# Reordering the step list of an attention and token-mixing kernel so that the steps of more batches are interleaved

## The chip, the cores and the metric

The kernel runs on one core of one Trainium2 chip. The metric is the device time of one execution in microseconds (us). Some words are used throughout. PE is TensorE's matrix unit and PEld its weight loads, DVE is VectorE, ACT is ScalarE, POOL is GpSimd, SP is SyncE. "Granted clock" is the share of full speed that the profile shows as granted to PE; in the clock records it is only ever 1.0 or 0.5 at any one moment. These records begin at about 34 us of the span before, and what lies before counts as full clock in every mean and row below. It was not: the eight `pq` transposes of batch 0 took 1.97 us, as at half clock (in the middle of the run they take 1.94 us at half clock). A timed run is 1.7 to 2.0 us longer than the span of instructions that its profile shows (one run 2.8), so spans are compared with spans and times with times. Runs are marked fast or slow (slow: over 1.5% above the fastest of the same kernel); only fast runs are compared.

## The reference

For each of 8 batches, 8 heads, 576 positions and head size 64, an attention with two parts is computed, and a token-mixing layer follows it.

```python
q_d, k_d, v_d = means over groups of 4 positions            # 144 coarse positions
out_d   = softmax(scale * q_d @ k_d.T) @ v_d                # coarse attention
out_up  = repeat(out_d, 4)                                  # back to 576 positions
local   = softmax(scale * q @ k.T where |i-j| < 4) @ v      # band attention
x       = (out_up + local) as (8, 576, 512)

wq, wk  = x @ w_q, x @ w_k                                  # 512 -> 64
W_tok   = wq @ wk.T / 8                                     # 576 x 576 per batch
out     = relu(W_tok @ x) @ w_out                           # 512 -> 512
```

## The kernel before

Each batch is cut into about forty small steps. A step issues a few instructions on one or several engines and hands its results on in a dictionary. The parts of a batch, in the order in which they depend on one another, with the names that the profile shows:

- `load_qk`, `load_v`: DMA of q, k, v. `cast_qk`, `cast_v`: casts to 16 bits, on GpSimd (for batch 0 q and k are cast on DVE and ACT).
- `tq`, `tk`, `tr`: transposes on PE (`pq`, `pk`, `pr`), copied to `qT`, `kT`. `sums`: sums over groups of 4 of `qT` and `kT`, on GpSimd.
- `mask`, `score`: band scores (`psc`), then `E = exp` on ACT. `av`: E times v (`pav`), normalised by DVE into `x`.
- `vd`, `cs`, `ca`: the coarse attention (`pv`, `pcs`, `pca`, with `Ec = exp` on ACT and `od` on DVE). `xt`, `odt`: transposes of x and od (`px`, `pod`).
- `wtd`, `wt`, `wkt`, `wks`, `m2`: the small products of the mixing layer (`pwd`, `pw`, `pwk`, `pws`, `pm`). `mx`: the mixing with relu (`pmx`, into `rmx`). `og`, `ol`: the output projections (`po`, `pol`), copied to `os`, `ol` and sent to memory.

Two things make the order of the steps matter. First, the program keeps the instructions of every engine in the order in which it issues them:

```python
class _InOrder:
    # ... cut ...
    def __getattr__(self, name):
        f_ = getattr(self._engine, name)
        return lambda *a, **k: self._tc.keep_in_program_order(f_(*a, **k))
```

Every instruction goes through the line with `keep_in_program_order`, which is why the profile gives L27 for nearly all of them; groups are told apart by their tiles. Second, the order is one list of (lag, step). In iteration i the step is run for batch i + lag:

```python
    ORDER = [
        (-2, "og1"), (-1, "wtd"), (0, "sums"), (1, "cast_qk"), (-1, "wt"), (0, "vd"), (0, "mask0"),
        (0, "score0"), (-1, "wks"), (2, "load_qk"), (1, "cast_v"), (0, "mask1"), (-1, "wkt"), (0, "score1"),
        (0, "mask2"), (0, "av0"), (-1, "m2"), (0, "av3"), (0, "score2"), (0, "av1"), (-1, "mx0"), (-1, "mx1"),
        (0, "av2"), (0, "cs0"), (-1, "mx2"), (0, "cs1"), (0, "av4"), (0, "weights"), (-1, "mx3"), (1, "tq"),
        (0, "ca0"), (2, "load_v"), (-1, "og0"), (0, "ca1"), (1, "tk"), (1, "tr"), (-1, "ol"), (0, "xt0"),
        (0, "xt1"), (0, "odt"),
    ]
    # ... cut ...
    for i in range(-3, B + 3):
        for lag, name in ORDER:
            if 0 <= i + lag < B and (i + lag, name) not in done:
                steps[i + lag][name]()
```

PSUM, where PE writes its results, has three rotating buffers for the large results and two for the small ones, so a PE group also waits until the group three before it has been read out (in the trace before, `pmx` waits seven times for DVE's `x` and six times for ACT's `E`, 4.1 and 3.6 us in all, and reads neither):

```python
    ps2 = ctx.enter_context(tc.tile_pool(name="ps2", bufs=3, space=bass.MemoryType.PSUM))
    ps1 = ctx.enter_context(tc.tile_pool(name="ps1", bufs=2, space=bass.MemoryType.PSUM))
```

The softmax here doesn't subtract the row's maximum and nothing guards it: scores larger than these inputs give would overflow.

## Time and profile before

| | before |
|---|---|
| time, median of the first three runs | 211.77 us (211.1 to 213.29) |
| span of the profiled run | 208.9 us |
| mean granted clock of that span | 0.909 |
| PE busy | 165.1 us of 208.9 |
| one batch in the middle of the run | about 22.3 us |

The page of the profiled run gives the busy time of each engine over the whole span, then rows with the busy share, in tenths, of 40 equal slices of the span (here 5.2 us each), then the chain of work that ended last, by engine. In the group line, the last column is the engine's idle time before that group and what ended it.

```profile
PE 165.1 (79%) x2768; PEld 110.7 (53%) x2768; DVE 106.5 (51%) x252; ACT 98.9 (47%) x141; POOL 114.9 (55%) x114
...
PE   0260889778998699959996899789986999699690
...
POOL 6005961998489907991299629970799167000000
PEclk9999999995799889985999699957998899859999
...
PE 59%; DVE 13%; POOL 8%; ACT 7%; SPq 6%; issue 3%; DMA 2%; POOLq 0%; ACTq 0%; DVEq 0%
...
L27 POOL TENSOR_TENSOR sum<-qT 128x1152 f32<-128x1152 f16 x8 | 16.9, 2114 | 37.7 <-ACT qT L27 37.7
```

PE is the busiest engine and the first of the chain, but the row of its clock has a dent once per batch: digits of 5 to 8 are slices in part of which the clock was halved. GpSimd idles 37.7 us for `qT`, because its sums stand right behind the transposes of their batch.

The view of chosen stretches has, for each stretch, its bounds and length, the busy time and the number of instructions of PE, PEld, DVE, ACT and POOL, then the granted clock, the DMA share and GB/s. The first two lines are two stretches of about a batch each; the others cut up one thin stretch and what follows it.

```profile
82.80:105.30 22.50, 20.08 (x346) 13.42 (x345) 11.94 (x24) 11.56 (x18) 14.19 (x14) 0.85 0.81 220
105.30:127.40 22.10, 19.51 (x351) 13.53 (x349) 12.01 (x25) 11.62 (x18) 15.97 (x14) 0.92 0.85 226
88.80:92.20 3.40, 1.61 (x56) 0.81 (x44) 2.96 (x6) 1.39 (x3) 3.40 (x3) 1.00 1.01 409
...
92.40:99.20 6.80, 6.24 (x55) 4.09 (x48) 3.38 (x8) 3.19 (x4) 2.60 (x2) 0.51 0.95 155
```

In the 3.40 us before 92.2, PE is busy 1.61 us, a share of 0.47. For the 6.8 us after it the clock is 0.51. The busy time of PE in a batch (20.08 and 19.51) thus contains work that ran at half speed.

The timeline of PE over this place shows start, duration, tile and count of each group, and in brackets the idle time before it and what ended that.

```profile
89.59 0.28 PE L27 MATMUL pmx<-wT,M 64*128 64x288 f16 x1 [0.59 <-ACT E L27]
90.11 0.29 PE L27 MATMUL pmx<-wT,M 64*128 64x288 f16 x1 [0.24 <-DVE M L27]
91.06 0.30 PE L27 MATMUL pmx<-wT,M 64*128 64x288 f16 x2 [0.67 <-DVE x L27]
91.29 0.32 PE L27 MATMUL pav<-v,E 64*64 64x65 f16 x16
91.91 0.59 PE L27 MATMUL pcs<-qd,kd 64*128 64x168 f16 x12 [0.29 <-DVE x L27]
...
94.88 1.94 PE L27 MATMUL pq<-id,q 128*128 128x128 f32 x8
```

Small groups stand here one behind another. Most wait for a PSUM buffer that DVE or ACT has yet to read out: the waits of 0.59, 0.67 and 0.29 us at 89.59, 91.06 and 91.91 ended with `E` and `x`, which read PSUM and are no inputs of these groups (the `pmx` at 90.11 waits for its input M). The eight `pq` transposes that follow take 1.94 us; at full clock in the same trace the eight `pk` transposes take 1.07 us.

### The profile page before, as it was taken

The page shows a single profiled execution, that of the slowest core. Times are in us where ns is not written, and L with a number is a line of the kernel's source. Part 1 is how long each engine was busy: PE and PEld are TensorE (multiplying, and loading weights), DVE is VectorE, ACT ScalarE, POOL GpSimd, SP SyncE. Part 2 cuts the span into 40 slices and gives each one's busy share as a digit, 9 for nine tenths or more (in the row PEclk, how much of TensorE's full clock was granted, in tenths as well). Part 3 has the DMA queues.
Part 4 walks back from the last instruction along what each step waited for, and adds up shares of the span by engine and source line. Part 5 has one row for each costly group of instructions (what it writes and reads, how often), then busy time and mean ns, then how long its engine had stood idle before and what let it go on. Part 6 is the DMA issues. An engine that isn't in the chain of part 4 may idle for free.

```text
span 208.9 us, 6392 instructions
## 1 busy us (share of the span) xinstructions
PE 165.1 (79%) x2768; PEld 110.7 (53%) x2768; DVE 106.5 (51%) x252; ACT 98.9 (47%) x141; POOL 114.9 (55%) x114
## 2 busy tenths in 40 slices
PE   0260889778998699959996899789986999699690
PEld 0240568546664476626763676356653776346330
DVE  4609464565345734574447445673458345644230
ACT  2170573445456445553574546544665346614231
POOL 6005961998489907991299629970799167000000
PEclk9999999995799889985999699957998899859999
DMA  6999999969969999898659995996220053002216
GB/s 199 335 178 334 387 162 284 311 128 295 301 121 317 369 186 245 250 346 137 180 145 386 154 221 147 346 240 134 104 104 3 0 151 107 0 3 100 100 38 213
DMA packets 53290, 40.53 MB, mean 194 GB/s; under 512 B 43984, under 2 KB 44048, under 8 KB 53264
## 3 DMA queue, kind: packets, MB, share of 16 engines
q1 hardware_dynamic: 53184, 40.12, 71.7%
q8 instruction: 21, 0.34, 0.7%
q14 instruction: 5, 0.04, 0.1%
q10 hardware_dynamic: 80, 0.03, 0.1%
HBM read 30.67 MB, written 9.44 MB: 192 GB/s over the span
## 4 chain that ended last, share of the span: by engine, by line
PE 59%; DVE 13%; POOL 8%; ACT 7%; SPq 6%; issue 3%; DMA 2%; POOLq 0%; ACTq 0%; DVEq 0%
PE po L27 14%; PE pq L27 7%; DVE x L27 6%; SPq L27 6%; PE pm L27 5%; PE pca L27 5%; PE psc L27 4%; PE pk L27 3%; PE pw L27 3%; PE px L27 3%; ACT Ec L27 2%; PE pws L27 2%; PE pav L27 2%; DMA w<-in_moe_w_q_dram 2%; POOL v L27 2%
## 5 line engine op out<-in xcount | busy, mean ns | idle before, releaser
L27 POOL TENSOR_TENSOR sum<-qT 128x1152 f32<-128x1152 f16 x8 | 16.9, 2114 | 37.7 <-ACT qT L27 37.7
L27 PE MATMUL po<-wo,rmx 128*128 128x512 f16 x128 | 34.9, 420 | 0.1
L27 POOL CAST v<-v 128x2560 f16<-128x2560 f32 x8 | 18.6, 2326 | 20.7 <-DMA w<-in_moe_w_q_dram 13.6
L27 ACT COPY os<-po 128x1024 f32<-128x1024 f32 x16 | 16.2, 1013 | 28.4 <-PE po L27 21.8
L27 DVE TENSOR_TENSOR x<-pav,rz 128x512 f16<-128x512 f32 x40 | 27.7, 692 | 1.4
L27 PE MATMUL pq<-id,q 128*128 128x128 f32 x64 | 15.8, 426 | 10.9 <-DVE q L27 9.4
L27 PEld LDWEIGHTS <-rmx 128*128 128x128 f16 x144 | 14.4, 107 | 16.2 <-issue 5.0
L27 ACT ACTIVATE E<-psc 128x928 f16<-128x928 f32 (+1 forms) x24 | 19.3, 806 | 4.5 <-PE psc L27 3.8
L27 POOL CAST q<-q 128x1152 f16<-128x1152 f32 x14 | 20.2, 1490 | 0.0
L27 POOL CAST k<-k 128x1152 f16<-128x1152 f32 x14 | 20.2, 1482 | 0.0
L27 PEld LDWEIGHTS pq<-id,q 128*128 128x128 f32 x64 | 12.4, 223 | 12.9 <-DVE q L27 9.4
L27 PE MATMUL pmx<-wT,M 64*128 64x288 f16 x64 | 11.2, 322 | 10.2 <-DVE x L27 4.1
L27 ACT ACTIVATE Ec<-pcs 128x1008 f16<-128x1008 f32 (+1 forms) x16 | 13.9, 873 | 10.8 <-PE pcs L27 10.8
L27 PE MATMUL pav<-v,E 64*64 64x65 f16 x640 | 15.1, 207 | 2.4 <-issue 0.9
L27 PEld LDWEIGHTS <-E 64*64 64x64 f16 x640 | 11.6, 116 | 9.3 <-issue 5.5
L27 DVE RECIPROCAL rc<-pca 128x8 f32<-128x8 f32 (+1 forms) x16 | 3.2, 203 | 25.1 <-PE pca L27 25.1
L27 POOL TENSOR_TENSOR sum<-kT 128x1152 f32<-128x1152 f16 x7 | 14.7, 2106 | 0.5
L27 DVE RECIPROCAL rz<-pav 128x8 f32<-128x8 f32 x40 | 8.1, 203 | 12.4 <-PE pav L27 12.2
L27 PEld LDWEIGHTS <-Ec 128*128 128x128 f16 x160 | 12.3, 122 | 4.1 <-issue 0.8
L27 ACT COPY qT<-pq 128x1024 f32<-128x1024 f32 x8 | 8.1, 1012 | 13.3 <-PE pq L27 13.3
L27 DVE TENSOR_TENSOR wT<-pw,wTd 128x576 f16<-128x576 f32 x8 | 6.1, 758 | 14.4 <-ACT wTd L27 12.9
L27 ACT ACTIVATE rmx<-pmx 128x576 f16<-128x576 f32 x16 | 10.3, 648 | 4.8 <-PE pmx L27 4.8
(79 smaller groups left out, 316.5 us busy)
## 6 DMA issues: line engine op xcount, KB each, us to landing
v<-in_v_dram SPq DMA_DIRECT2D x80, 128.0 KB, 6.2
q<-in_q_dram SPq DMA_DIRECT2D x8, 1152.0 KB, 7.4
k<-in_k_dram SPq DMA_DIRECT2D x8, 1152.0 KB, 10.9
out_dram<-os SPq DMA_DIRECT2D x16, 512.0 KB, 3.3
wo<-in_moe_w_out_dram SPq DMA_DIRECT2D x2, 512.0 KB, 10.5
out_dram<-ol SPq DMA_DIRECT2D x8, 128.0 KB, 2.6
w<-in_moe_w_q_dram SPq DMA_DIRECT2D x1, 128.0 KB, 4.6
w<-in_moe_w_k_dram SPq DMA_DIRECT2D x1, 128.0 KB, 4.4
```

The lines of the kernel that those rows point to most:

```text
L27: return lambda *a, **k: self._tc.keep_in_program_order(f_(*a, **k))
```

## The change

The intent is to give every group of PE work of another batch to stand between it and its consumer, so that PE, DVE, ACT and GpSimd wait less for each other. No instruction is added or removed. The step list is rewritten: the output projections now come one to three batches further behind the casts than before, the other steps lie in between, and the lags run from +2 to -4 instead of +2 to -2.

```diff
     ORDER = [
-        (-2, "og1"), (-1, "wtd"), (0, "sums"), (1, "cast_qk"), (-1, "wt"), (0, "vd"), (0, "mask0"),
-        (0, "score0"), (-1, "wks"), (2, "load_qk"), (1, "cast_v"), (0, "mask1"), (-1, "wkt"), (0, "score1"),
-        (0, "mask2"), (0, "av0"), (-1, "m2"), (0, "av3"), (0, "score2"), (0, "av1"), (-1, "mx0"), (-1, "mx1"),
-        (0, "av2"), (0, "cs0"), (-1, "mx2"), (0, "cs1"), (0, "av4"), (0, "weights"), (-1, "mx3"), (1, "tq"),
-        (0, "ca0"), (2, "load_v"), (-1, "og0"), (0, "ca1"), (1, "tk"), (1, "tr"), (-1, "ol"), (0, "xt0"),
-        (0, "xt1"), (0, "odt"),
+        (-1, "mask2"), (-1, "score2"), (-4, "ol"), (-2, "vd"), (-2, "av4"), (-2, "cs0"), (-3, "m2"),
+        (-2, "cs1"), (-2, "av2"), (-4, "og0"), (-3, "mx1"), (-2, "ca0"), (-3, "mx0"), (0, "tq"), (-2, "ca1"),
+        (0, "tk"), (-1, "sums"), (-2, "xt0"), (1, "cast_qk"), (2, "load_qk"), (-3, "mx3"), (-2, "odt"),
+        (-1, "mask0"), (-1, "score0"), (-2, "xt1"), (1, "load_v"), (0, "cast_v"), (0, "weights"), (-3, "mx2"),
+        (0, "tr"), (-2, "wtd"), (-1, "mask1"), (-1, "score1"), (-1, "av0"), (-2, "wt"), (-1, "av3"),
+        (-3, "og1"), (-2, "wkt"), (-1, "av1"), (-2, "wks"),
     ]
-    for i in range(-3, B + 3):
+    for i in range(-6, B + 6):
```

In three steps `if i == 0` became a test whether the tile exists already, so that a tile shared by sister steps is made by whichever of them comes first.

More of the change, by code (lines that the diff above doesn't have):

```diff
@@ L376, in f_ @@
                 Ec = EcS[b % 2]
-                if i == 0:
+                if "rc" not in g_:
                     g_["rc"] = big.tile([128, 2, 2, 4], FP32, name="rc", tag="rc")
@@ L414, in f_ @@
             def f_():
-                if i == 0:
+                if "rz" not in g_:
                     g_["rz"] = big.tile([128, NW, 2, 4], FP32, name="rz", tag="rz")
@@ L441, in f_ @@
             def f_():
-                if i == 0:
+                if "xT" not in g_:
                     g_["xT"] = big.tile([128, 4, 2, 290], FP16, name="xT", tag="xT")
```

## The prediction

> **What bounds the kernel now.** In the middle of the run a batch takes about 22.3 us (stretches 82.8 to 105.3 and 105.3 to 127.4 of the view by stretches). TensorE (PE) is busy 20.1 and 19.5 us of these, VectorE about 12, ScalarE 11.6, GpSimd 14 to 16. PE bounds it, but not at its own speed. Each batch has a thin stretch: around the pav, pmx and pcs groups PE waits for VectorE's x or ScalarE's E, and its busy share falls to 0.28, 0.29, 0.65 in three successive microseconds (89 to 92). The granted clock then drops to 0.5 for 3.4 or 6.8 us, by turns (period means 0.92 and 0.85); the pq transposes and an output projection fall in it (8 pq 1.94 us, 8 pk at full clock 1.07). [...]
>
> **What the change does.** Nothing is added or removed; the same 2768 matmuls stand in another order. Each scores, av, mx, coarse and projection group now has work of another batch, ready an iteration earlier, between it and its consumer. Transposes no longer wait for the same iteration's casts; GpSimd's sums wait for a qT that is an iteration old (now it idles 6 to 8 us per batch for it).
>
> **Cost.** Per batch PE's work at full clock, an estimate from start-to-start times in full-clock stretches, is 17.4 us (busy 19.5 to 20.1 less half of the throttled part). GpSimd needs 15.9. DMA: loading one batch takes 15 to 16.5 us from its first packet to its last, its outputs some 3 more, so 18 to 19 if they do not overlap. I estimate 18 to 19 us a batch in place of 22.3, 2 to 2.5 of it from the clock, 1.5 from waits. Half-clock stretches should become rare in the middle.
>
> Given back at the ends: first, GpSimd casts q and k of batch 1 before v of batch 0, and PE has transposes of batch 1 queued ahead of most of batch 0: after the first scores it should idle from about 15 to about 30 us. And the last batch drains over four thin iterations (last pq to end some 53 us; now 47.5). Together 8 to 10 us lost, against six or seven periods times 4 saved.
>
> **Prediction.** Stringing the new queue orders with the trace's durations gives a span near 191 us, so about 193 us timed (timed runs lie 2 to 3 us above the span). Range 185 to 203. Faster by over 2%: 0.94; within: 0.05; slower: 0.01.
>
> **What would show it.** Mean granted clock in the middle 0.93 or more; period between successive pq groups 18 to 19.5 us; GpSimd over 80% busy in the middle, its wait for qT gone; PE busy time down to about 150 us; PE idle 13 us or more before 35 us; loads done by about 130 us instead of 146.
>
> **What would make it wrong.** DMA: if q, k, v loads and outputs slow each other, the period goes to 20 to 21 and the time over 203; then PE or GpSimd waits for in_q or in_v show. If thin windows remain (three rotating PSUM buffers still make PE wait), the clock stays near 0.9 and the time is near 200. If the clock never drops and DMA overlaps, 183.

22.3 us less 2 to 2.5 (clock) and 1.5 (waits) is 18.3 to 18.8 us a batch, and 208.9 us less six or seven times 4 plus 8 to 10 is a span of 189 to 195, with 191 from the strung queue orders.

## The result

| | before | after |
|---|---|---|
| time, median (lowest to highest, 4 runs each) | 211.44 us (210.28 to 213.29) | 194.03 us (193.46 to 196.35) |
| span of the profiled run | 208.9 us | 191.6 us |
| mean granted clock | 0.909 | 0.979 |
| PE busy | 165.1 us | 153.3 us |
| PE idle (span less busy) | 43.8 us | 38.3 us |

The ratio of after to before is 0.919, with a 95% interval of 0.909 to 0.929, so the changed kernel is faster. Here and below a ratio is the mean time of one kernel's fast runs over that of the other's of the same rounds, so it is not quite the ratio of the medians quoted.

The page of the profiled run after the change, the same lines (a slice is now 4.8 us):

```profile
PE 153.3 (80%) x2768; PEld 100.0 (52%) x2768; DVE 111.1 (58%) x252; ACT 99.3 (52%) x141; POOL 116.0 (61%) x114
...
PE   0071009789899998999999989998999899988890
...
POOL 7000599989979999999999997297459000000000
PEclk9999999859999999999999999999999999999998
...
PE 38%; SPq 32%; POOL 11%; issue 7%; ACT 3%; DMA 3%; DVE 3%; POOLq 0%; ACTq 0%
```

The matmuls are the same 2768, yet PE is busy 11.8 us less: the dents in the clock row are gone but for one near the start. PE's share of busy time has hardly moved (79% to 80%) while the time fell by 8%. So the busy share said little here of how near the kernel was to its limit: busy time stretches when the clock is halved (eight `pq` take 1.94 us in place of 1.06).

The view of stretches, after: the start, three stretches of about a batch each in the middle, and the end.

```profile
0.00:28.60 28.60, 4.66 (x20) 3.67 (x20) 7.44 (x52) 8.35 (x8) 10.81 (x24) 1.00 1.06 303
77.50:96.20 18.70, 17.84 (x343) 11.14 (x341) 12.69 (x25) 11.64 (x17) 18.31 (x18) 1.00 1.03 268
96.20:114.80 18.60, 17.67 (x344) 11.67 (x344) 11.68 (x24) 11.60 (x18) 18.37 (x18) 1.00 0.94 263
114.80:134.40 19.60, 18.66 (x349) 12.01 (x349) 12.76 (x25) 11.73 (x18) 13.03 (x12) 1.00 0.79 196
170.00:191.60 21.60, 15.12 (x128) 7.62 (x126) 6.54 (x11) 7.37 (x11) 0.00 (x0) 0.98 0.36 130
```

The three stretches of the middle run at a clock of 1.00, and PE is idle for only 0.9 us of each. In the first of them GpSimd is busy for 18.31 of 18.70 us. In the last 21.6 us PE is busy for 15.12 us alone: that is the drain of the last batch.

The chain has turned: SPq, the issue of DMAs on SyncE, has 32% of it in place of 6%. Step by step, the chain runs through load issues from the start to about 37 us and from 53 to 81 us, then through GpSimd to 96 us and through PE to the end. That raises the question whether the loads bound the new kernel in its first 80 us; it is taken up in experiment 4.

The timeline of PE in the middle, after:

```profile
110.66 0.32 PE L27 MATMUL pav<-v,E 64*64 64x65 f16 x16
110.91 1.90 PE L27 MATMUL po<-wo,rmx 128*128 128x512 f16 x8
112.75 0.30 PE L27 MATMUL pmx<-wT,M 64*128 64x288 f16 x2
...
113.90 0.30 PE L27 MATMUL pmx<-wT,M 64*128 64x288 f16 x2 [0.27 <-DVE rmx L27]
114.83 1.06 PE L27 MATMUL pq<-id,q 128*128 128x128 f32 x8 [0.64 <-DVE od L27]
```

A whole output projection of an older batch (1.90 us of PE work) stands between the `pav` groups and the `pmx` groups that used to wait for one another, and `pq` takes 1.06 us in place of 1.94.

Where the 17.3 us of span come from can be read off the starts of the `pq` groups in the two timelines:

| batch of `pq` | 0 | 1 | 2 | 3 | 4 | 5 | 6 | 7 | end |
|---|---|---|---|---|---|---|---|---|---|
| before, us | 9.4 | 28.4 | 49.7 | 72.0 | 94.9 | 116.8 | 139.6 | 161.4 | 208.9 |
| after, us | 9.3 | 29.0 | 41.8 | 58.1 | 76.7 | 96.3 | 114.8 | 134.4 | 191.6 |

Up to `pq` of batch 3 the change gains 13.9 us; part of that is no real gain, since the new order brings the transposes forward and puts older work off. The four periods from batch 3 to batch 7 gain 13.1 us (89.4 to 76.3, so 22.4 to 19.1 each). From the last `pq` to the end it loses 9.7 us (47.5 to 57.2), because more of the older work is still to be done.

The view of these four periods together, before and then after:

```profile
71.99:161.37 89.38, 79.30 (x1384) 53.80 (x1385) 47.86 (x99) 46.36 (x68) 60.32 (x53) 0.88 0.77 200
```

```profile
58.11:134.39 76.28, 72.88 (x1385) 47.39 (x1385) 50.76 (x99) 46.81 (x69) 68.78 (x61) 1.00 0.93 244
```

For the same work PE is busy 6.4 us less (79.3 to 72.9), which is the clock's part, and idle 6.7 us less (10.1 to 3.4), which is the waits' part. So in the middle the two parts are about equal, 1.6 and 1.7 us a batch; the split is rough, as the ends of matmuls are modelled.

The start shows the price of the change. First the timeline of PE, then that of ACT, over the same time:

```profile
14.61 0.37 PE L27 MATMUL psc<-id,neg 64*128 64x224 f16 x2
28.63 0.43 PE L27 MATMUL psc<-qT,kT 64*64 64x56 f16 x16 [13.65 <-DVE kT L27]
```

```profile
14.29 1.01 ACT L27 COPY kT<-pk 128x1024 f32<-128x1024 f32 x1 [1.19 <-PE pk L27]
25.48 1.04 ACT L27 CAST wo<-wo 128x1024 f16<-128x1024 f32 x1 [10.18 <-DMA wo<-in_moe_w_out_dram]
26.82 1.05 ACT L27 CAST wo<-wo 128x1024 f16<-128x1024 f32 x1 [0.30 <-DMA wo<-in_moe_w_out_dram]
27.77 0.38 ACT L27 COPY qT<-pr 128x128 f32<-128x128 f32 x1
```

PE stands still for 13.65 us. It waits for the last column of `kT`, whose sister copy `qT<-pr` sits on ACT behind the casts of the output weights (step `weights`), and those wait for their DMA.

### The profile page after: what moved, and what is told of

It reads as the page before. It is cut to its first block, busy times and chain, and to the rows that moved or that the text cites. A ratio compares the mean times of both kernels' runs of the same rounds, so it can differ in the third digit from the quotient of the medians.

```text
span 191.6 us, 6402 instructions
## 1 busy us (share of the span) xinstructions
PE 153.3 (80%) x2768; PEld 100.0 (52%) x2768; DVE 111.1 (58%) x252; ACT 99.3 (52%) x141; POOL 116.0 (61%) x114
## 2 busy tenths in 40 slices
DMA packets 53291, 40.54 MB, mean 212 GB/s; under 512 B 43984, under 2 KB 44048, under 8 KB 53264
## 4 chain that ended last, share of the span: by engine, by line
PE 38%; SPq 32%; POOL 11%; issue 7%; ACT 3%; DMA 3%; DVE 3%; POOLq 0%; ACTq 0%
SPq L27 32%; PE po L27 9%; POOL sum L27 4%; PE pm L27 4%; PE psc L27 4%; DMA v<-in_v_dram 3%; PE px L27 3%; ACT os L27 3%; PE pw L27 2%; PE pav L27 2%; POOL q L27 2%; PE pq L27 2%; PE pmx L27 2%; PE pol L27 1%; PE pcs L27 1%
## 5 line engine op out<-in xcount | busy, mean ns | idle before, releaser
L27 ACT COPY os<-po 128x1024 f32<-128x1024 f32 x16 | 16.2, 1012 | 28.1 <-PE po L27 19.6
L27 PE MATMUL po<-wo,rmx 128*128 128x512 f16 x128 | 30.5, 380 | 0.1
L27 POOL CAST v<-v 128x2560 f16<-128x2560 f32 x8 | 18.6, 2325 | 8.2 <-DMA v<-in_v_dram 5.1
L27 ACT ACTIVATE E<-psc 128x928 f16<-128x928 f32 (+1 forms) x24 | 19.5, 812 | 6.9 <-PE psc L27 6.1
L27 PE MATMUL psc<-qT,kT 64*64 64x58 f16 (+1 forms) x640 | 10.0, 197 | 13.6 <-DVE kT L27 13.6
L27 PE MATMUL pq<-id,q 128*128 128x128 f32 x64 | 11.2, 333 | 11.7 <-DVE q L27 9.3
L27 PEld LDWEIGHTS <-rmx 128*128 128x128 f16 x144 | 12.7, 98 | 14.4 <-ACT rmx L27 0.9
L27 PEld LDWEIGHTS <-kT 64*64 64x64 f16 x640 | 7.4, 112 | 17.9 <-DVE kT L27 13.9
L27 DVE COPY xT<-px 128x1160 f16<-128x1160 f16 x16 | 12.2, 761 | 7.0 <-PE px L27 7.0
L27 PEld LDWEIGHTS pq<-id,q 128*128 128x128 f32 x64 | 9.0, 172 | 12.6 <-DVE q L27 9.3
L27 ACT ACTIVATE Ec<-pcs 128x1008 f16<-128x1008 f32 (+1 forms) x16 | 13.7, 862 | 2.4 <-PE pcs L27 2.4
L27 DVE TENSOR_SCALAR rmx<-pmx 128x576 f16<-128x576 f32 x16 | 12.0, 752 | 3.9 <-PE pmx L27 3.9
L27 PEld LDWEIGHTS <-E 64*64 64x64 f16 x640 | 9.8, 110 | 5.0 <-ACT E L27 2.5
L27 POOL TENSOR_TENSOR kd<-sum 128x160 f16<-128x160 f32 x28 | 11.8, 453 | 0.5
```

## The experiments

Theory C, the clock: most of the gain is that the thin stretch is gone, so PE's clock is no longer halved. Rival W, the waits: the gain is that the engines wait less for each other, and the clock is a bystander. A second question is which resource bounds the new kernel, and a third what the start and the depth of the interleaving are worth. Each run was profiled and timed in three rounds beside the kernel before on the same chip; the sessions ran on different chips (8, 15, 7 and 1, where the kernel before had medians of 210.94, 211.13, 211.33 and 209.84 us).

### 1. Useless work in the thin stretch of the kernel before

Nine matmuls whose result nobody reads were put into each batch's thin stretch, with the old order kept. PE gets more work, so if only work and waits count, this is no faster.

```diff
+        def fill(n):                    # not for batch 0
...
+                p_ = psm(name="pfl")
+                for _ in range(n):
+                    pe.matmul(p_, id16, wo16[:, 0, :], start=True, stop=True)
...
-   (0, "av1"), (-1, "mx0"), (-1, "mx1"), (0, "av2"), (0, "cs0"), (-1, "mx2"), (0, "cs1"),
+   (0, "av1"), (-1, "fl0"), (-1, "mx0"), (-1, "fl1"), (-1, "mx1"), (0, "av2"), (-1, "fl2"),
+   (0, "cs0"), (-1, "mx2"), (-1, "fl3"), (0, "cs1"),           # 2, 3, 2, 2 matmuls
```

> The kernel before, its order kept, with 9 useless 128x128 by 512 matmuls per batch (2, 3, 2, 2; about 0.217 us each at full clock, so about 2 us a batch and 14 us in all) put into the thin stretch where PE waits for x and E. Clock theory (the half clock after the thin window costs 2 to 2.5 us a batch): the half-clock stretches become rarer, mean clock over 0.94, and the kernel gets FASTER than before although it does more work: 203 to 207 us. Rival (the gain of the change is only waits overlapped, the clock is a bystander): the filler hides partly in the waits and adds the rest: 212 to 220 us.

The result is correct. The time is 204.35 us (202.97 to 205.64) against 210.94 for the kernel before (209.24 to 214.62), ratio 0.970 (0.962 to 0.977). The page of this run, its clock row, and then its timeline of PE at the place shown for the kernel before:

```profile
PE 167.9 (83%) x2831; PEld 106.7 (53%) x2831; DVE 109.3 (54%) x252; ACT 99.1 (49%) x141; POOL 114.9 (57%) x114
...
PEclk9999999995899999999999999999999999999997
```

```profile
87.73 0.61 PE L27 MATMUL pfl<-wo,id 128*128 128x512 f16 x2
...
88.92 0.29 PE L27 MATMUL pmx<-wT,M 64*128 64x288 f16 x1 [0.24 <-DVE M L27]
89.14 0.82 PE L27 MATMUL pfl<-wo,id 128*128 128x512 f16 x3
...
93.82 1.06 PE L27 MATMUL pq<-id,q 128*128 128x128 f32 x8 [0.42 <-POOL v L27]
```

The 63 added matmuls are 13 to 14 us of work at full clock (an estimate: one more matmul in a `pfl` group takes 0.21 us), and the kernel is 6.6 us faster by the medians. The clock stays at full speed through the middle (1.00 in the view from 72.3 to 135.7 us) and `pq` takes 1.06 us. So the clock is no bystander, and rival W as stated falls: no step was moved ahead; only the gaps were filled. It gives nearly 40% of the gain of the change (6.6 of 17.4 us). This does not say that the remainder is waits alone, since the fillers themselves cost PE time. Between `pq` of batch 3 and of batch 7 (83.5 us) PE is busy 79.9 us, of which the 36 fillers are about 7.6 (by the same estimate), so the old work takes about 72 us in place of 79.3; PE's idle time falls from 10.1 to 3.6 us. The fillers thus mostly took the place of waits, and the whole of the clock's part was won.

### 2. The output projections put together again: a faulty and a mended build

To take the spread of the heavy groups away while the depth stays, the two output projections were placed together. The first build also moved `ol`, behind a `mx` step that overwrites the columns which it reads.

```diff
-   (-4, "ol"), ... (-4, "og0"), ... (-1, "av0"), (-2, "wt"), (-1, "av3"), (-3, "og1"),
+   ... (-1, "av0"), (-2, "wt"), (-4, "og0"), (-3, "og1"), (-4, "ol"), (-1, "av3"),
```

> The changed kernel, all batch distances kept, but the three output projection groups (og0, og1, ol) stand together in one place after wt instead of spread over the iteration. Theory (it is PE work spread between the groups that wait for VectorE and ScalarE that keeps the clock up and the waits hidden): half-clock stretches come back, mean clock 0.93 or less, the period grows to 20 us or more, time 203 to 213 us. Rival (what helps is that producers are an iteration earlier): stays within 2% of 194.

The result is wrong (relative error 0.237), and the time 214.62 us (212.07 to 215.89), ratio 1.014 (1.005 to 1.024). The mended build leaves `ol` where it was:

```diff
-   (-4, "og0"), (-3, "mx1"), ... (-1, "av0"), (-2, "wt"), (-1, "av3"), (-3, "og1"),
+   (-3, "mx1"), ... (-1, "av0"), (-2, "wt"), (-4, "og0"), (-3, "og1"), (-1, "av3"),
```

> The run with the output projections together, mended: there the shared tail projection stood behind a step that overwrites its input, and the result was wrong. Here ol keeps its place and og0 and og1 stand together after wt, og0 with nothing of a later batch written into its columns before. Expected as in that run, less the tail: half-clock stretches back, mean clock 0.92 to 0.95, 205 to 213 us, and a correct result. If only the misplaced ol made it slow: within 3% of 194.

It is correct, and takes 211.46 us (209.55 to 212.99, two of four runs slow), ratio of the fast runs 0.997 (0.986 to 1.009). The whole gain is gone. Two of its stretches of about a batch each, with the clock in the third column from the right:

```profile
78.20:101.60 23.40, 20.60 (x349) 13.69 (x350) 13.47 (x27) 11.80 (x18) 23.08 (x22) 0.93 0.85 211
...
122.90:147.40 24.50, 20.66 (x349) 13.67 (x349) 14.38 (x27) 11.84 (x18) 11.82 (x10) 0.92 0.53 142
```

The half-clock stretches are back, and `pq` groups are 19.8 to 24.4 us apart. But this profile fell in a slow run (212.83 us), so I take no sizes from it. The two fast runs had a mean granted clock of 0.961 and 0.963, the four of the changed kernel 0.979 to 0.981. That is about 8 us more at half clock (an estimate: twice the missing share times the span), which can cost at most 4 of the some 15 us lost. Most of the loss is therefore not the clock; that it is waits fits PE's idle time in the slow profile (49.3 us, 38.3 in the changed kernel), but no fast profile of this build shows it. In this build, interleaving deeply gives nothing by itself.

### 3. The output projections spread in the kernel before

The counterpart: the old order and depth, but the two projections of the batch two before are placed behind `av1` and `av2`, in the thin stretch.

```diff
-   (-2, "og1"), (-1, "wtd"), ... (0, "av1"), (-1, "mx0"), (-1, "mx1"), (0, "av2"), ... (-1, "og0"),
+   (-1, "wtd"), ... (0, "av1"), (-2, "og0"), (-1, "mx0"), (-1, "mx1"), (0, "av2"), (-2, "og1"), ...
```

> The kernel before, one part of the change alone: its two output projections, taken one batch later, stand in the thin stretch (after av1 and after av2), everything else as before, no step of scores, casts or coarse attention earlier. If filling the thin stretch with any PE work is what the change does: the half clock goes, as in the filler run, and 200 to 206 us. If the places that the projections leave (between pq, the coarse attention and its evacuations) become thin in their turn, so that spreading needs the deeper batch distances: half clock stays and 210 us or more; an estimate from the durations says 220.

It is correct and slower: 222.4 us median of four runs, of which two are fast (219.81 and 220.67), against 209.84 for the kernel before. In the profiled run, which is fast, `pq` groups are 22.4 to 26.4 us apart in the middle and PE waits elsewhere. One line of its timeline of PE and, from its view of waits, one with the total, the number and the longest:

```profile
105.56 0.42 PE L27 MATMUL pwd<-odT,wqk 128*128 128x72 f16 x8 [1.51 <-DVE odT L27]
```

```profile
PE pwd L27 <- DVE odT L27: 10.4, 8, 1.5
```

`po` used to stand between the end of the coarse attention and the `pwd` product that needs its transposed result. With `po` taken away, PE waits there once in every batch. The half clock did not stay, as the second reading above expected: the granted clock is 0.950, higher than before (0.909), and PE is busy 159.9 us in place of 165.1. But it is idle 58.9 us in place of 43.8. So here the waits alone make the kernel slower, although the clock is better. The four builds form a square:

| | projections together or as before | projections spread |
|---|---|---|
| old depth | before: 211 us | run 3: 220 us (two fast runs) |
| new depth | mended run 2: 210 us (fast runs) | after: 194 us |

My reading is that the heavy groups can be moved into the thin stretch without opening another gap only where the deeper interleaving lets other work cover the old place. One placement was tried for each half; in these two builds neither half of the change is worth anything alone.

### 4. What bounds the new kernel

Three kernels add load to one resource of the changed kernel each, and one takes some away.

PE: the nine useless matmuls per batch again, now in one place of the new order.

```diff
-   (-2, "wt"), (-1, "av3"),
+   (-2, "wt"), (-2, "fill"), (-1, "av3"),     # 9 matmuls, not for batch 0
```

> Changed kernel, PE made dearer: 9 useless 128x128 by 512 matmuls in one place per batch of the last seven (about 2 us a batch, 14 in all, the same amount as in the filler run of the kernel before). If PE at full clock bounds the changed kernel from about 58 us on, nearly all of it shows: 203 to 209 us. If DMA or GpSimd bounds it: under 199.

The time is 210.47 us (209.37 to 210.86) against 211.13 for the kernel before, ratio 1.000 (0.992 to 1.007). That is 16.4 us more than the median of the changed kernel in its own runs for 13 to 14 us of added work, at a granted clock of 0.991. In the old order the same work made the kernel faster; here every microsecond counts in full. Between `pq` of batch 3 and of batch 7 the run takes 86.4 us in place of 76.3, for some 7.6 us of added work. It is even 1.5 us above the range expected (203 to 209); PE's idle time in these periods also rises, from 3.4 to 5.2 us, and I did not look further. PE bounds the middle of the new kernel.

GpSimd: the first addition of the sums of q is done twice.

```diff
-                add(s_, t4[:, :, 0:2], t4[:, :, 2:4], op=ALU.add)
+                for _ in range(2 if i == 0 else 1):
+                    add(s_, t4[:, :, 0:2], t4[:, :, 2:4], op=ALU.add)
```

> Changed kernel, GpSimd made dearer: the first addition of the q sums is done twice, 2.1 us more per batch (its work a batch from about 15.4 to 17.5 us). If PE bounds: 194 to 198. If GpSimd bounds: 206 or more.

The time is 196.7 us (195.7 to 197.79), ratio 0.936 (0.926 to 0.947). GpSimd got 16.4 us more to do (116.0 to 132.4 us busy) and the kernel took 2.7 us longer. Between `pq` of batch 3 and of batch 7 GpSimd is busy 75.2 of 76.6 us here, and 68.8 of 76.3 in the changed kernel, so it had room although it was at 98% in two of the batches. My reading is that the lead of its steps over those that use them lets its work run late. Here a busy share of 98% over two batches (PE 95%) did not make an engine the bound.

DMA, more: each output block is sent twice (8.4 MB more).

```diff
-                sp.dma_start(out[b, t0:t0 + 256].rearrange("(m p) d -> p m d", p=128), os_)
+                for _ in range(2):
+                    sp.dma_start(out[b, t0:t0 + 256].rearrange("(m p) d -> p m d", p=128), os_)
```

> Changed kernel, DMA made dearer: each 512 KB output transfer is issued twice (about 1.05 MB and 2.8 us of the 16 DMA engines more per batch). If DMA has slack behind the PE: 194 to 198, some 1.5 us of it from the last transfer alone. If the loads bound the middle, the prediction's fear: 204 or more, with GpSimd waiting for in_q and in_v; an estimate from the durations says 207.

The time is 210.05 us (208.63 to 213.53, one slow), ratio 0.996 (0.986 to 1.006). Up to the last `pq` nothing is lost: it starts at 135.3 us, against 134.4. Then comes the loss. The timeline of GpSimd in this run, and its stretch after the last `pq`:

```profile
152.97 2.32 POOL L27 CAST v<-v 128x2560 f16<-128x2560 f32 x1 [8.03 <-DMA out_dram<-os]
```

```profile
135.30:160.00 24.70, 20.52 (x344) 13.61 (x344) 12.12 (x24) 12.72 (x19) 16.28 (x14) 0.86 0.66 194
```

The last v is cast at 152.97 us, in place of 134.76 in the changed kernel, and the profile names the transfer of an output as what ended GpSimd's wait; that the load of v queued behind the doubled outputs is my reading of this. PE then runs thin and the clock falls to 0.86 in that stretch; from the last `pq` to the end the run takes 72.2 us in place of 57.2. How the loss divides between bytes, issues, waits and clock was not separated.

DMA, less: only half of v is loaded and used twice, which is wrong (relative error 1.13; 35.30 MB moved in place of 40.54).

```diff
-        v32 = st[b]["v32"] = big.tile([128, NW, H, D], FP32, name="v32", tag="v32")
+        v32 = st[b]["v32"] = big.tile([128, NW, H // 2, D], FP32, name="v32", tag="v32")
...
-            pool.tensor_copy(v16[:, :, :, 0:64], g_["v32"])
+            for p in range(2):
+                pool.tensor_copy(v16[:, :, 4 * p:4 * p + 4, 0:64], g_["v32"])
```

> Changed kernel with half of v loaded (4 of 8 heads; both halves are cast from the same 4, so the result is wrong on purpose; GpSimd's cast is two instructions of half the size). About 5 MB and 4 us of DMA a batch less, PE, VectorE and ScalarE the same. If PE alone bounds the changed kernel from 58 us on: 190 to 195. If the loads hold it as well: 187 or less.

The time is 193.7 us (192.89 to 194.99), ratio 0.924 (0.916 to 0.931), the same as the changed kernel within the noise. Its chain, by engine:

```profile
PE 64%; DVE 11%; DMA 10%; ACT 6%; issue 5%; SPq 3%; ACTq 0%; DVEq 0%
```

The load issues have left the chain (32% to 3%), PE has taken their place, and the end has not moved. So in the first 80 us of the changed kernel the loads run level with PE: they appear on the chain, but taking away half of v gains nothing, and adding DMA work late in the queue costs much (210.05 us with the outputs doubled). The number of load issues was not changed here, only their bytes.

### 5. The start

The cause that the trace of the changed kernel gives for the idle start is the step `weights`. In one build it was moved behind `tr`, so that ACT copies `qT<-pr` first.

```diff
-   (0, "cast_v"), (0, "weights"), (-3, "mx2"), (0, "tr"), (-2, "wtd"),
+   (0, "cast_v"), (-3, "mx2"), (0, "tr"), (0, "weights"), (-2, "wtd"),
```

> The changed kernel with the weights step moved behind tr, so that ScalarE's two copies of the output weights, which wait for their DMA until 25.5 and 26.8 us, no longer stand ahead of the copy of qT's last column that the first scores need. If the idle of PE from 14.7 to 28.6 us is made by that wait: first scores at about 16 us, pq of batch 1 at 24 to 25 us instead of 29.0, and 2 to 4 us off the time (190 to 192). If GpSimd's casts and the loads of batch 1 set the start, as the prediction said: scores early, but pq of batch 1 still after 27 us (its casts end at 23.6 for q and 27.0 for k), and under 1.5 us off.

It is correct: 195.67 us median (192.99 to 203.76, two of four slow), ratio of the fast runs 0.918 (0.910 to 0.926), the same as that of the changed kernel within the noise. The long wait for `kT` is gone and `pq` of batch 1 starts 4.5 us earlier (24.5 us), but then PE waits 7.0 us for GpSimd's cast of q of batch 1, and by `pq` of batch 3 the run is 1.2 us behind the changed kernel. So the wait is as the first reading above had it, and the time as the second. That profile fell in a slow run (span 195.5), so I don't compare its later stretches. The fast times alone say that the head start is worth nothing in the end.

The cast of q and k was moved from the middle of the list, for the next batch, to the head of the next iteration's list:

```diff
-   (-1, "mask2"), (-1, "score2"), ... (-2, "xt0"), (1, "cast_qk"), (2, "load_qk"),
+   (0, "cast_qk"), (-1, "mask2"), (-1, "score2"), ... (-2, "xt0"), (2, "load_qk"),
```

> The changed kernel with only cast_qk put back: the cast of a batch stands in the same iteration as its transposes, at its start, instead of one iteration ahead. If the casts ahead are part of the gain (PE no longer waits for them), PE's wait of pq for GpSimd's k grows by over 1 us a batch and the time to 199 or more. If they are not, within 3 us of the changed kernel; an estimate from the durations says 1 to 3 us slower.

It is correct and slower: 203.29 us median, two fast runs (200.54 and 202.96); the other two took 203.62 and 207.18. I had expected much less of a loss. The timeline of GpSimd shows where it starts:

```profile
40.98 2.32 POOL L27 CAST v<-v 128x2560 f16<-128x2560 f32 x1 [7.94 <-DMA v<-in_v_dram]
43.24 2.84 POOL L27 CAST q<-q 128x1152 f16<-128x1152 f32 x2
```

GpSimd now takes v of batch 1 ahead of q and k of batch 2, and stands still 7.94 us for its load. PE runs out of transposes, the clock is halved from 40.2 to 50.5 us, and `pq` of batch 3 starts 6.5 us later than in the changed kernel. So the place that the change gives to these casts pays: that it casts q and k of a batch before v of the batch ahead of them is worth this much at the start.

A hand-written order of the first 56 steps, with the casts of batch 1 on DVE and ACT and with the output weights loaded and cast late, was to shorten the start:

```diff
-            cast("q", dve.tensor_copy if b == 0 else pool.tensor_copy)
-            cast("k", act.copy if b == 0 else pool.tensor_copy)
+            cast("q", dve.tensor_copy if b <= 1 else pool.tensor_copy)
+            cast("k", act.copy if b <= 1 else pool.tensor_copy)
...
+    for b, name in FIRST:            # 56 steps, then the loop as before
+        steps[b][name]()
+        done.add((b, name))
```

> Changed kernel with another start, an attempt to beat both: the first 56 steps are written out by hand. Batch 0 does not wait for its lag but runs through to the mix products before transposes of batch 2 follow; q and k of batch 1 are cast by VectorE and ScalarE (idle then), the output weights are loaded behind q, k, v of batch 2's turn and cast late. From batch 3 on the order is the changed one. Theory: the start is bound by loads and casts, so PE can gain only by doing more of batch 0 and 1 in it: pq of batch 3 at 55 to 57 us, pq of batch 7 at 129 to 131 instead of 134, 186 to 190 us timed. Rival (only the full-clock PE work after 58 us counts, the start cannot be shortened): within 2 us of 194.

It is correct: 195.0 us (192.74 to 195.44), ratio 0.921 (0.913 to 0.929). It did not beat the change. `pq` of batch 3 starts at 57.0 us, 1.1 us earlier than in the changed kernel, but that of batch 4 at 77.1 us, 0.4 us later: 13.7 us of half clock (at 40.1 and at 50.4 us) lie before it, against 6.8 us in the changed kernel.

Last, PE was kept busy during the idle start with 80 useless matmuls behind `tr` of batch 0, to have the clock full when real work comes:

```diff
-   (0, "tr"), (-2, "wtd"),
+   (0, "tr"), (0, "warm0"), (-2, "wtd"),      # 80 matmuls of 256 columns, batch 0 only
```

> Changed kernel with 80 useless matmuls of 256 columns (about 0.11 us each warm) put on PE behind tr of batch 0, into its idle from 14.7 to 28.6 us, so that the clock is full when the work of 28.6 to 43.8 us comes, which ran at half clock. If PE is what holds up the first two batches: pq of batch 3 3 to 5 us earlier and 189 to 191 us. If loads and casts hold them up: the clock is full and the time within 1.5 us of the changed kernel's.

It is correct: one fast run of 194.73 us, and three slow ones of 200.87 to 206.02. In the profiled run, the fast one, the timeline of PE has:

```profile
14.49 10.82 PE L27 MATMUL pfl<-neg,id 128*128 128x256 f16 x80
...
28.56 0.39 PE L27 MATMUL psc<-qT,kT 64*64 64x56 f16 x16 [3.06 <-DVE kT L27]
28.88 1.97 PE L27 MATMUL pq<-id,q 128*128 128x128 f32 x8
```

The first 18 fillers started 213 ns apart and the later ones 109 ns; the clock record of this run begins between them, at 18.4 us. So in this run the time before the record begins ran at half clock. The fillers ended too early: after a wait of 3.06 us the clock was halved again, and `pq` took 1.97 us as without them. The half-clock stretch came at 38.9 us all the same. Of the work from 28.6 to 43.8 us, which the expectation puts at half clock, the changed kernel ran 33.6 to 37.0 us at full clock and the remainder at half (`pq` at 28.99 and 41.78 us took 1.97 and 1.95 us). Nothing was won, and since the clock was not full when the real work came, the run does not decide its question.

No run beat the changed kernel beyond the noise.

## Why the prediction was right

**The time.** It said 193 us, 185 to 203, faster with 0.94. The median is 194.03, and the ratio 0.919 excludes "within 2%".

**Clock and waits.** It said 2 to 2.5 us a batch from the clock and 1.5 from waits. The four middle periods show about 1.6 and 1.7: both parts are there, the clock's is smaller than said, and the sum is 3.3 in place of about 4. Over the whole span PE's busy time fell 11.8 us, to 153.3 (it said about 150), for the same matmuls; its idle time fell only 5.5 us, because up to `pq` of batch 3 there is more of it (27.5 us in place of 24.0). Experiment 1 shows the clock's part by itself: adding work to the old order makes it faster. Experiment 3 shows that the clock alone is not enough: there PE's waits grew by more than the better clock gave. In experiment 2 most of the loss is not the clock either. So neither theory C nor rival W holds alone. In the middle the granted clock is 1.00, more than the 0.93 asked for.

**Where the sum was lucky.** It was six or seven periods of 4 us less 8 to 10 us at the ends. From `pq` of batch 0 to 7 the gain is 27.0 us, close to seven times 4, but the first three periods gave 13.9 of it (4.6 each, partly work put off) and the last four 3.3 each. That these differences cancel was not foreseen.

**How thin is too thin.** What the clock records show is this: the half-clock stretches of the kernel before last 3413 or 6827 ns by turns, seven in the run and 37.5 us together; after the change the record has one, of 6827 ns, at 37.0 us. (One more begins in each record in the last 1.1 us of the span, 4.5 and 4.0 us after the last matmul.) The others follow stretches in which PE pauses several times and briefly: in the 3.41 us before them no gap is longer than 0.86 us, and in the one shown above none is 0.7 us long. From the matmul intervals of the two traces I worked out PE's busy share in each 3413 ns (the length of the shorter half-clock stretch) from the start of the clock record to the last matmul: in the kernel before, drops follow shares of 0.48 to 0.67, and full clock was kept after 0.63 and more; in the changed kernel it was kept after 0.73 and lost after 0.69. The two ranges overlap between 0.63 and 0.69, so this measure does not tell when the clock falls.

**The period.** It said 18 to 19.5 us; the four periods are 18.6, 19.6, 18.6 and 19.6. It lies at the upper edge of what was said, and I did not look for the cause of the alternation.

**What bounds it.** The prediction gave PE's work as 17.4 us a batch, GpSimd's as 15.9 and the DMA's as 18 to 19 if nothing overlaps, and left open which would hold. The runs say PE in the middle: 17.7 to 18.7 us busy of 18.6 to 19.6, and added PE work costs its full length. GpSimd is over 80% busy in the first two of the three batches, as it said, and its wait for `qT` (37.7 us) is no longer among its waits, the longest of which is now its first load:

```profile
POOL q L27 <- DMA q<-in_q_dram: 16.1, 1, 16.1
```

In the third batch its share falls to 66%, because there is no further q and k to cast.

**The named danger, DMA.** It said 203 us or more if the transfers slow each other. They didn't in full: the chain has load issues on it up to 81 us, but halving v gained nothing, and the last packets of v come at about 133.5 us (it said 130; before 145.7). Doubling the outputs shows how near the danger was.

**The ends.** It said that 8 to 10 us are given back at both ends together. The drain from the last `pq` took 57.2 us (it said 53; before 47.5), so 9.7 us were lost there alone. At the start PE stood still 13.65 us before 35 us, as it said (13 or more). But the cause it named, GpSimd casting batch 1 before v of batch 0, with transposes of batch 1 queued first, was not what ended that wait: it was ACT, held by the casts of the output weights. With those out of the way, the cause it named takes their place (PE waits 7.0 us for the cast of q in the run with `weights` moved), so it was a second cause just behind the first. This is the weak step of the prediction: the size was right and the releaser was not.

**What stays open.** Three builds change the start and none ends earlier. In their profiled runs (one of them slow) a part of what they gain goes into additional half-clock stretches between 28 and 61 us, and two of them had slow runs more often (two and three of four). Another reason may be that the loads run level with PE up to 81 us, so that a head start is lost by then; that is argued from the chain and was not tested. How thin a stretch must be for the clock to fall was not found either, nor why the mended build of experiment 2 waits.

## What to carry to other kernels

When PE is the bound but its clock is not full, look at the row of the clock first, and for the few microseconds before each dent: many waits below a microsecond there cost as much through the clock as by themselves in this case (1.6 and 1.7 us a batch), and putting ready work of another batch between the waiting groups paid for both. Such an order needs depth and placement together; one without the other gained nothing or lost here. A cheap test is to fill the thin stretch with useless matmuls: if the kernel gets faster, as here with 63 of them (210.94 to 204.35 us), the clock was part of the cost.
